# Value loads of the first attention tiles on either of two DMA queues, and new numbers in a hand-written planner

## The chip, the cores and the metric

The kernel runs on one core of a Trainium2 chip. The metric is device time in microseconds (us) of one execution. TensorE (PE) multiplies, VectorE (DVE) and ScalarE (ACT) work elementwise, GpSimd (POOL) helps them, SyncE (SP) only issues DMAs. ACT can issue DMAs too: the issue then stands in ACT's own instruction stream.

## The reference

```python
# attention: 4 x 8 heads x 576 tokens x 64; heads 0-3 see the last 32 tokens, heads 4-7 every 32nd token
scores = where(mask, scale * q @ k.T, -1e9); attn = softmax(scores); x = attn @ v
x = x.transpose(0, 2, 1, 3).reshape(2304, 512)
h = x @ w_in;  r = maximum(h, 0);  x = (s * r * r + b) @ w_out          # MLP 1, 512 -> 2048 -> 512
h = x @ w_in2; g = where(h >= 1, h, where(h <= -1, 0, (h + 1)**2 / 4))  # MLP 2
out = g @ w_out2
...
```

Everything is float32. The weights arrive as float64 and are taken apart on the chip.

## The kernel before, in words

**Tiling.** The 2304 tokens make six units of 384. Attention comes in tiles: "strided" ones (three per batch entry) and "local" ones of 256 tokens. Tiles 0 to 4 give unit 0 its tokens (0, 1, 2 strided, 3, 4 local); tile 5 is local and serves unit 1. One tile is a chain: scores on PE, maximum and subtraction on DVE, `Exp` on ACT (`sm` or `sx`), sum and reciprocal on DVE, a product on DVE or POOL, four transposes on PE, a copy `pt` on ACT or DVE, the value products on PE, and the result as a high part `xh` (ACT) and a remainder `xl` (DVE).

**MLP.** `hidden` multiplies a unit by a block of w_in, three products per tile (high by high, low by high, high by low), `output` multiplies the activated block by w_out. Each weight block of 512 KB is loaded into a `raw` or `pp` buffer, decoded (ACT L461, DVE L463 and L465) and split (ACT L442, DVE or POOL L482). A step of unit 0 needs two blocks. So the first 30 us are attention of tiles 0 to 4 beside the first loads, and the rest is a dense stream of matrix products.

**The order.** Nothing is ordered by hand after the first loads. `Issue.draw` plays the program forward with a table of costs and random due times, `order` keeps the best of 96 draws, and `emit` writes each engine's instructions in the order of the planned starts. An operation may name several engines; the planner takes the one that is free first. While PE is planned to wait before 45 us, `Pulse.run` adds dummy products (`busy`, L703 before), at most 8 in a place, to keep it active.

**Loads.** `load` (L589) issues the attention's DMAs. Up to `CALM` = 32 us of planned time, `emit` also makes each DMA on SP wait for an earlier one, so that about 2.5 planned us of bytes are under way. Apart from that the built program hands eight DMA semaphores, DMAHW0 to DMAHW7, to the DMAs in turn, in the order in which `emit` writes them; a DMA whose semaphore is still in use waits for the DMA eight places ahead of it to land. `EARLY` fixes the order in which the first tiles' loads enter the plan. Rows (queries and keys) go to `xh`/`xl` buffers, the early tiles' values to weight buffers that are still empty: tile 0 `w0hx`, tile 1 `w0lx`, tile 3 `w1hx` and `w1lx`, tile 2 `w0hx`, tile 4 `w0lx` and `w1hx`.

Of the kernel before, what the change touches and what calls it, by code (L numbers as in the profile page):

```python
# [31 lines left out]
KT = QT + STRIDE  # L32
# [12 lines left out]
FILL, MOST = 45.0, 8  # L45
# [30 lines left out]
LATENCY = 0.12  # L76
DMA_LATENCY = 2.0
DMA_ISSUE, SHORT = 0.45, 0.64
LATE, LATE_FROM, LATE_TO = 1.5, 22.0, 40.0
PIECE, PIECE_BYTE, DEEP = 0.008 / 16, 0.0435e-3 / 16, 1.0  # L80
BEGIN = {"sp": 0.7, "act": 1.4, "dve": 0.5, "pool": 6.4, "pe": 5.2}
WINDOW, PHASE, COOL, HEAT = 3.413, 2.3, 0.58, 0.9
BLOCK, FETCH, FETCH_AT, FETCH_LONG = 256, 4.5, 1.5, 1.3
CALM, FLIGHT = 32.0, 2.5
EARLY = (('rows', 0), ('rows', 1), ('w0', 0), ('vals', 0), ('rest', 0), ('rows', 3), ('vals', 1), ('rows', 4), ('vals', 3), ('vals', 2), ('vals', 4), ('w0', 1))

# [1 line left out]
class Buf:  # L88


    def __init__(self, ring, make):
        self.ring, self.make = ring, make
        self.writers, self.readers, self.users = [], [], []
        self.tile, self.left, self.end, self.near = None, 0, 0.0, 0.0
# [20 lines left out]

class Pulse:

    def __init__(self):
        self.end, self.full, self.used, self.count, self.began, self.fetched = PHASE + WINDOW, True, WINDOW, 86, 0.0, None

    def upto(self, t):
        while t >= self.end:
# [11 lines left out]
    def run(self, o, free, at, d):  # L134
        n = 0
        if at < FILL and o.fills is not None and at > free:
            self.upto(free)
            one = 0.213 if self.full else 0.427
            n = min(int(0.85 * (at - free) / one), MOST)
            self.spend(free, n * one)  # L140
        self.upto(at)
        if not self.full:
            d *= 1.85
        left = BLOCK - self.count % BLOCK
        self.count += o.count + 2 * n
        if o.count + 2 * n >= left:
            t = at + d * max(left - 2 * n, 0) / max(o.count, 1)
            self.fetched = t
            wait = max(self.began + FETCH - t, 0.0) if at < FILL else 0.0
            self.began, d = t + wait, d + wait  # L150
        self.spend(at, d)
        return n, d

# [5 lines left out]
class Issue:  # L159
# [70 lines left out]
    def draw(self, seed):  # L230
        rng = np.random.default_rng(seed)
        for ring in self.rings:
            ring.taken = []
        for o in self.ops:
            o.due = o.base + JITTER * rng.standard_normal()
            for b in o.bufs:
                b.end = b.near = 0.0
        free, pe, flight = {"port": 0.0, "dma": 0.0, "slow": 0.0}, Pulse(), []
        for o in self.ops:
            o.wait, o.ready = len(o.deps), 0.0  # L240
            for x in o.engs:
                free[x[0]] = BEGIN.get(x[0], 0.0)
            for b in o.bufs:
                b.left = len(b.users)
        pool = [o for o in self.ops if not o.wait]
        done, took = [], {}

        def room(o):
            t, more = 0.0, {}
            for b in o.allocs:  # L250
                n = len(b.ring.taken) + more.get(b.ring, 0) - b.ring.bufs
                more[b.ring] = more.get(b.ring, 0) + 1
                if n >= 0:
                    if n >= len(b.ring.taken) or b.ring.taken[n].left:
                        return None
                    t = max(t, b.ring.taken[n].near if o.engs[0][0] == "pe" else b.ring.taken[n].end)
            return t

        while pool:
            best = None  # L260
            for o in pool:
                t = room(o)
                if t is None:
                    continue
                for e, d, _, *more in o.engs:
                    at = max(free[e], o.ready, t)
                    if more and e != "pool" or "port" in more:
                        at = max(at, free[more[0]] - DEEP * (e == "sp"))
                    if e == "sp" and at < CALM:
                        at = max([at, *(end for line, end in flight if free["dma"] - line >= FLIGHT)])  # L270
                    key = (at, o.due, o.n, d)
                    if best is None or key < best[0]:
                        best = (key, o, e, d, t)
            if best is None:
                return np.inf, None
            (at, *_), o, e, d, t = best
            _, _, lag, *more = next(x for x in o.engs if x[0] == e)
            pool.remove(o)
            n = 0
            if e == "pe":  # L280
                n, d = pe.run(o, max(free[e], t), at, d)
                if pe.fetched is not None and at < FILL:
                    free["slow"], pe.fetched = max(free["slow"], pe.fetched + FETCH_AT) + FETCH_LONG, None
            took[o] = at, e, n
            free[e] = at + d
            end = at + d + lag
            if more and more[0] == "port":
                free["port"] = at + d
            elif more:
                free["dma"] = max(free["dma"], at + more[2]) + more[1]  # L290
                free["slow"] = max(free["slow"], at + more[2]) + more[1]
                end = max(at + d, free["dma"], free["slow"]) + lag + LATE * (e == "sp" and LATE_FROM < at < LATE_TO)
                if e == "sp" and at < CALM:
                    flight.append((free["dma"], end))
                    flight = flight[-12:]
            for b in o.allocs:
                b.ring.taken.append(b)
            for b in o.bufs:
                b.left -= 1
                b.end = max(b.end, end + LATENCY)  # L300
                b.near = max(b.near, at + d if e == "pe" else end + LATENCY)
            for q in o.succ:
                q.wait -= 1
                q.ready = max(q.ready, at if o in q.behind else at + d if q.engs[0][0] == e == "pe" else end + LATENCY)
                if not q.wait:
                    pool.append(q)
            done.append(o)
        assert len(done) == len(self.ops)
        return free["pe"], took
# [20 lines left out]
def sparse_attention_two_mlps(ctx: ExitStack, tc: tile.TileContext, loc, strd, w_ins, w_outs, fixed, out):  # L330
# [36 lines left out]
    class Tokens:  # L367
        def __init__(self, tag):
            self.tag, self.bufs = tag, {}
# [64 lines left out]
    def dma(n, piece, count=1, late=0.0, issue=DMA_ISSUE):  # L434
        return ("sp", issue * count, DMA_LATENCY + late, "dma", moved(n, piece), 0.0)
# [125 lines left out]
    def value_rows(src):  # L561
        (step, _), (one, n) = src.ap
        return bass.AP(tensor=src.tensor, offset=src.offset, ap=[[step, 64], [54 * step, 2], [one, n]])
# [11 lines left out]
    def is_early(i):  # L575
        return first_token(i) < U0[1]
# [9 lines left out]
            tag = "kb"  # L586
        return buf(wp if tag[0] == "w" else sp, tag, [128, 512], F32, BUFS.get(tag, MS // 2))

    def load(i, y, parts, size, piece):  # L589
        first = len(w_loads) > max(HOLD) and not held  # L590
        o = op(lambda e: [e.dma_start(out=f(), in_=x) for f, x in parts], [dma(size, piece, len(parts), issue=SHORT if len(a_line) > 2 else DMA_ISSUE)], part=[y],  # L591
               line=a_line, after=[w_loads[k] for k in HOLD] if first else ())
        if first:
            held.append(o)
            o.behind += tuple(w_loads[k] for k in HOLD)
        if i == 0 and not made[0]:
            w0_line[:] = [o]
        if is_early(i):
            w1_line[:] = [o]
        return o  # L600
# [56 lines left out]
    def vals(i):  # L657
        kind, b, d = tiles[i]
        if kind == "l":
            vs = [room(i, "vals") for _ in range(2)]  # L660
            for pos in range(2):
                for g in range(2):
                    load(i, vs[pos], [(lambda pos=pos, g=g: vs[pos].tile[half(g), :],
                                       loc[2 * d + pos][32 * g:32 * g + 64, 512 + 4 * KT:LW])], 128 * 1024, 2048)
            return vs
        vb_ = room(i, "vals")
        v4 = lambda: vb_.tile.rearrange("p (g n) -> p g n", g=2)
        if d < 2:
            for j in range(2):
                load(i, vb_, [(lambda j=j: v4()[j * 64:j * 64 + 64], value_rows(strd[b, 2 * d + j][:, VC:SW]))], 128 * 1024, 1024)  # L670
        else:
            src = strd[b, 4]
            parts = [(lambda: v4()[0:18, 0], strd[b, 3][108:126, VC:SW]), (lambda: v4()[18:36, 0], src[0:18, VC:SW]),
                     (lambda: v4()[0:64, 1], src[18:82, VC:SW]),
                     (lambda: v4()[64:118, 0], strd[b, 0:3, 108:126, VC:SW])]
            for j in range(2):
                load(i, vb_, parts[2 * j:2 * j + 2], 64 * 1024, 1024)
        return [vb_]

    def bring(i):  # L680
# [766 lines left out]
```

## Time and profile before

| | us |
|---|---|
| median of 3 runs | 823.38 (820.41 to 823.86) |
| profiled execution, its own time | 822.9 |
| its span, first to last instruction | 820.8 |
| TensorE busy in the span | 809.3 (99%) |

The profiled execution is 0.5 us under the median, and 2.1 us of it lie outside the span. The table says that PE is nearly always busy; dummy products count as busy, so the start has to be read in order of time.

### The profile page before, as it was taken

The page shows a single profiled execution, that of the slowest core. Times are in us where ns is not written, and L with a number is a line of the kernel's source. Part 1 is how long each engine was busy: PE and PEld are TensorE (multiplying, and loading weights), DVE is VectorE, ACT ScalarE, POOL GpSimd, SP SyncE. Part 2 cuts the span into 40 slices and gives each one's busy share as a digit, 9 for nine tenths or more (in the row PEclk, how much of TensorE's full clock was granted, in tenths as well). Part 3 has the DMA queues.
Part 4 walks back from the last instruction along what each step waited for, and adds up shares of the span by engine and source line. Part 5 has one row for each costly group of instructions (what it writes and reads, how often), then busy time and mean ns, then how long its engine had stood idle before and what let it go on. Part 6 is the DMA issues. An engine that isn't in the chain of part 4 may idle for free.

```text
span 820.8 us, 17686 instructions
## 1 busy us (share of the span) xinstructions
PE 809.3 (99%) x6295; PEld 783.3 (95%) x6295; DVE 629.0 (77%) x1316; ACT 517.9 (63%) x1057; POOL 103.7 (13%) x206
## 2 busy tenths in 40 slices
PE   7999999999999999999999999999999999999998
PEld 4689998999999999999999999999999999999998
DVE  5798439787777477888889988997477987466966
ACT  3486446565666576657686778855476854667553
POOL 3132103352221022221120000000000000000000
PEclk9999999999999999999999999999999999999999
DMA  7795365989777468989899999788988789878882
GB/s 238 237 335 179 101 217 195 316 267 312 259 256 267 163 227 306 329 320 332 293 315 320 300 395 351 253 251 286 296 256 254 249 255 297 288 249 255 252 271 93
DMA packets 105523, 218.23 MB, mean 266 GB/s; under 512 B 14196, under 2 KB 27868, under 8 KB 105436
## 3 DMA queue, kind: packets, MB, share of 16 engines
q1 hardware_dynamic: 95196, 180.41, 67.6%
q0 software_dynamic: 10240, 36.71, 11.9%
q8 instruction: 50, 0.82, 0.4%
q14 instruction: 37, 0.30, 0.1%
HBM read 170.93 MB, written 46.14 MB: 264 GB/s over the span
## 4 chain that ended last, share of the span: by engine, by line
PE 93%; DMA 4%; SPq 2%; DVE 0%; ACT 0%; issue 0%; ACTq 0%
PE acc L1119 8%; PE acc L1121 8%; PE acc L1120 8%; PE h L871 8%; PE h L872 8%; PE h L873 8%; PE side L1121 6%; PE side L1120 6%; PE side L1119 6%; PE acc L871 4%; PE acc L873 4%; PE acc L872 4%; PE h L1121 3%; PE h L1119 3%; PE h L1120 3%; SPq L591 2%
## 5 line engine op out<-in xcount | busy, mean ns | idle before, releaser
L871 PE MATMUL h<-xh,w0h 128*128 128x384 f32 x192 | 65.6, 342 | 0.4 <-ACT xh L442 0.4
L872 PE MATMUL h<-xl,w0h 128*128 128x384 f32 x192 | 64.6, 337 | 1.2 <-DVE xl L854 1.2
L871 PE MATMUL h<-xh,w0hx 128*128 128x384 f32 x192 | 65.6, 342 | 0.0
L873 PE MATMUL h<-xh,w0l 128*128 128x384 f32 x192 | 64.5, 336 | 0.1
L872 PE MATMUL h<-xl,w0hx 128*128 128x384 f32 x192 | 64.4, 335 | 0.0
L873 PE MATMUL h<-xh,w0lx 128*128 128x384 f32 x192 | 64.4, 335 | 0.0
L512 POOL DMA_DIRECT2D dw<-pp x60 | 43.5, 725 | 157.9 <-DVE pp L510 127.4
L903 ACT ACTIVATE t<-h 128x384 f32<-128x384 f32 x50 | 24.4, 489 | 39.0 <-PE h L873 38.6
L915 DVE TENSOR_TENSOR gg<-t,gg 128x384 fp32r<-128x384 f32 x39 | 21.6, 555 | 24.9 <-ACT gg L442 24.9
L872 PEld LDWEIGHTS h<-xl,w0h 128*128 128x128 f32 x192 | 36.1, 188 | 1.8 <-DVE xl L854 1.8
L871 PEld LDWEIGHTS h<-xh,w0h 128*128 128x128 f32 x192 | 36.0, 188 | 1.1 <-ACT xh L442 0.8
L871 PEld LDWEIGHTS h<-xh,w0hx 128*128 128x128 f32 x192 | 36.0, 188 | 0.5
L873 PEld LDWEIGHTS h<-xh,w0l 128*128 128x128 f32 x192 | 36.0, 188 | 0.4 <-DVE w0l L482 0.4
L872 PEld LDWEIGHTS h<-xl,w0hx 128*128 128x128 f32 x192 | 36.1, 188 | 0.0
L873 PEld LDWEIGHTS h<-xh,w0lx 128*128 128x128 f32 x192 | 36.0, 188 | 0.0
L442 ACT ACTIVATE gg<-w1h 128x384 fp32r<-128x384 f32 x48 | 24.9, 524 | 15.6 <-PE acc L1121 6.2
L871 PE MATMUL acc<-gg,w1h 128*128 128x384 f32 (+1 forms) x96 | 33.4, 348 | 0.2 <-DVE xl L854 0.2
L1165 DVE TENSOR_TENSOR gg<-w1h,gg 128x384 fp32r<-128x384 f32 x48 | 26.4, 554 | 8.6 <-ACT gg L442 8.1
L871 PE MATMUL acc<-gg,w1hx 128*128 128x384 f32 (+1 forms) x96 | 33.0, 344 | 0.0
L873 PE MATMUL acc<-gg,w1lx 128*128 128x384 f32 (+1 forms) x96 | 32.2, 336 | 0.0
L873 PE MATMUL acc<-gg,w1l 128*128 128x384 f32 (+1 forms) x96 | 32.2, 336 | 0.0
L872 PE MATMUL acc<-gg,w1h 128*128 128x384 f32 x96 | 32.2, 335 | 0.0
(626 smaller groups left out, 2796.2 us busy)
## 6 DMA issues: line engine op xcount, KB each, us to landing
dw<-pp POOLq DMA_DIRECT2D x60, 512.0 KB, 4.9
w0h<-dw SPq DMA_DIRECT2D x84, 256.0 KB, 3.8
w0l<-dw SPq DMA_DIRECT2D x84, 256.0 KB, 3.9
w0hx<-dw SPq DMA_DIRECT2D x84, 256.0 KB, 3.1
w0lx<-dw SPq DMA_DIRECT2D x84, 256.0 KB, 3.2
raw<-in_w_ins SPq DMA_DIRECT2D x30, 512.0 KB, 4.6
raw<-in_w_outs SPq DMA_DIRECT2D x28, 512.0 KB, 6.0
kb<-dw SPq DMA_DIRECT2D x56, 256.0 KB, 4.4
```

Of the source, the lines that this page charges most:

```text
L442: e.activation(out=out, in_=in_, func=AF.Copy)
L512: op(lambda e: e.dma_start(out=dw[o][i][qs].rearrange("q p w n -> p q (w n)"), in_=y.tile[:, 0:nq].bitcast(F32).rearrange("p q w n -> p q ...
L591: o = op(lambda e: [e.dma_start(out=f(), in_=x) for f, x in parts], [dma(size, piece, len(parts), issue=SHORT if len(a_line) > 2 else DMA_ ...
L871: e.matmul(out=acc, lhsT=wh, rhs=ah, start=first, stop=False)
L872: e.matmul(out=acc[:, 0:al.shape[1]], lhsT=wh, rhs=al, start=False, stop=False)
L873: e.matmul(out=acc, lhsT=wl, rhs=ah, start=False, stop=last)
L903: op(lambda e: e.activation(out=c(t), in_=c(p), func=AF.Relu), [act(n)], [p], [t])
L915: op(lambda e: e.tensor_tensor(out=c(gl), in0=c(t), in1=c(gh).bitcast(F32), op=SUB), [pool(n)] + [dve2(n)], [t, gh], [gl])
L1119: e.matmul(out=dst, lhsT=wh, rhs=ah, start=opens and first, stop=False, skip_group_check=not opens)
L1120: e.matmul(out=dst[:, 0:al.shape[1]], lhsT=wh, rhs=al, start=False, stop=False, skip_group_check=not opens)
L1121: e.matmul(out=dst, lhsT=wl, rhs=ah, start=False, stop=last, skip_group_check=not opens)
L1165: op(lambda e, g=g, hi=hi, lo=lo: e.tensor_tensor(out=lo.tile[:, 0:n], in0=g.tile, in1=hi.tile[:, 0:n].bitcast(F32), op=SUB), [dve2(n)], [ ...
```

## The change

Value loads of tiles that reach into unit 0 may go to ACT as well as to SP, as long as the first loads are under way (`held` is still empty); the planner picks. The order in which loads enter the plan stays. The wait of at most `DEEP` us for the DMA line now also holds for ACT's issues; the limit on bytes under way still counts SP's alone. In the planner's table, bytes on the lagging DMA engine are planned 1.2 times up to 34 us; a late landing is planned as 0.8 us between 32 and 80 us, before as 1.5 us between 22 and 40; and the fetch of PE's instructions now takes its turn on the lagging engine when a DMA is planned behind it.

```diff
-LATE, LATE_FROM, LATE_TO = 1.5, 22.0, 40.0
+LATE, LATE_FROM, LATE_TO = 0.8, 32.0, 80.0
...
-BLOCK, FETCH, FETCH_AT, FETCH_LONG = 256, 4.5, 1.5, 1.3
+BLOCK, FETCH, FETCH_AT, FETCH_LONG = 256, 1.7, 1.0, 1.3
+SLOW, SLOW_TO = 1.2, 34.0
...
-            self.fetched = t
-            wait = max(self.began + FETCH - t, 0.0) if at < FILL else 0.0
-            self.began, d = t + wait, d + wait
+            if self.fetched is not None and at < FILL:
+                self.free["slow"] = max(self.free["slow"], self.fetched) + FETCH_LONG
+                self.coming, self.fetched = self.free["slow"] + FETCH, None
+            wait = max(self.coming - t, 0.0) if at < FILL else 0.0
+            d += wait
+            self.fetched = t + wait + FETCH_AT
...
-                        at = max(at, free[more[0]] - DEEP * (e == "sp"))
+                        at = max(at, free[more[0]] - DEEP * (e in ("sp", "act")))
...
-                free["slow"] = max(free["slow"], at + more[2]) + more[1]
+                if pe.fetched is not None and pe.fetched <= at < FILL:
+                    free["slow"] = max(free["slow"], pe.fetched) + FETCH_LONG
+                    pe.coming, pe.fetched = free["slow"] + FETCH, None
+                free["slow"] = max(free["slow"], at + more[2]) + more[1] * (SLOW if at < SLOW_TO else 1.0)
...
-    def load(i, y, parts, size, piece):
+    def load(i, y, parts, size, piece, also=False):
         first = len(w_loads) > max(HOLD) and not held
-        o = op(lambda e: [e.dma_start(out=f(), in_=x) for f, x in parts], [dma(size, piece, len(parts), issue=SHORT if len(a_line) > 2 else DMA_ISSUE)], part=[y],
+        ways = [dma(size, piece, len(parts), issue=SHORT if len(a_line) > 2 else DMA_ISSUE)]
+        if (also and is_early(i)) and not held:
+            ways.append(("act", *ways[0][1:]))
+        o = op(lambda e: [e.dma_start(out=f(), in_=x) for f, x in parts], ways, part=[y],
```

The four calls of `load` in `vals` pass `True` for `also`. What this makes of the two queues' streams is shown at three places (the last number of a name is the buffer's).

SP before, from the last rows of tile 3 to the second weight block; `xh3` and `xl3` are tile 4's rows, `w...` are values, `raw_22` is the weight block:

```order
L591 DMA xl4_11_269<-in_loc 128x896
L591 DMA w0lx_12_279<-in_strd 64x2x256 x2
L591 DMA xh3_13_303<-in_loc 128x896
L591 DMA xl3_14_309<-in_loc 128x896
L591 DMA w1hx_15_339<-in_loc 64x512 x2
L591 DMA w1lx_16_366<-in_loc 64x512 x2
L591 DMA w0hx_17_414<-in_strd 18x256 x2
L591 DMA w0hx_17_414<-in_strd 64x256
L591 DMA w0hx_17_414<-in_strd 54x1x256
L591 DMA w0lx_18_471<-in_loc 64x512 x2
L591 DMA w1hx_19_499<-in_loc 64x512 x2
L457 DMA raw_22_528<-in_w_ins 128x512
```

The same stretch of SP after the change, with the semaphores that each DMA waits for:

```order
L601 DMA xl4_11_273<-in_loc 128x896 [waits DMAHW2_49]
L601 DMA xh3_13_282<-in_loc 128x896 [waits DMAHW0_49]
L601 DMA xl3_14_310<-in_loc 128x896 [waits DMAHW6_49,DMAHW1_49]
L601 DMA w1hx_15_340<-in_loc 64x512 [waits DMAHW7_49,DMAHW2_49]
L601 DMA w1lx_16_393<-in_loc 64x512
L601 DMA w0hx_17_420<-in_strd 64x256
L601 DMA w0hx_17_420<-in_strd 54x1x256 [waits DMAHW3_49]
L464 DMA raw_22_523<-in_w_ins 128x512 [waits DMAHW4_49]
```

Between tile 4's last rows and the weight block stand four DMAs where there were twelve.

ACT after the change, from the second half of tile 3's `w1lx` to the `Exp` of tile 2; `sm_50` is tile 3, `pt_37` tile 1, `sx_42` tile 2:

```order
L601 DMA w1lx_16_393<-in_loc 64x512 [waits DMAHW5_49]
L601 DMA w0hx_17_420<-in_strd 18x256 [waits DMAHW6_49]
L601 DMA w0hx_17_420<-in_strd 18x256 [waits DMAHW7_49]
L601 DMA w0lx_18_428<-in_loc 64x512 [waits DMAHW1_49]
L793 ACTIVATE sm_50_350<-sm_50_350 128x4x128 [waits DVE_49,Activation_49,Pool_49]
L601 DMA w0lx_18_428<-in_loc 64x512 [waits DMAHW3_49]
L449 ACTIVATE pt_37_432<-h_36_431 128x512 [waits PE_49]
L601 DMA w1hx_19_443<-in_loc 64x512 [waits DMAHW5_49]
L601 DMA w1hx_19_443<-in_loc 64x512 [waits DMAHW7_49]
L793 ACTIVATE sx_42_402<-sx_42_402 128x4x128 [waits DVE_49,Pool_49]
```

Before, ACT held only the three activations here, in the order `pt_37`, `sx_42`, `sm_50`. Eleven of its instructions are now DMA issues, the first ahead of all softmax work and the others between the softmax steps of tiles 0 to 2, and tile 5's scores stand ahead of the first `hidden` on PE where they stood inside it.

## Rows read from the trace of the kernel before

**Rows 1.** Windows of the whole span: busy us of each engine, clock, DMA share, GB/s.

```profile
core 0: us, PE busy (x) PEld busy (x) DVE busy (x) ACT busy (x) POOL busy (x), PEclk, DMA share, GB/s
32.00:50.00 18.00, 15.81 (x201) 12.99 (x202) 15.31 (x31) 12.66 (x27) 4.35 (x7) 1.00 1.00 335
...
700.00:800.00 100.00, 100.00 (x578) 100.00 (x577) 68.07 (x133) 64.30 (x129) 0.00 (x0) 1.00 0.83 261
```

**Rows 2.** TensorE in order of time: start, length, what, [idle before <- releaser].

```profile
19.78 0.62 PE L769 MATMUL acc<-xl 64*32 64x64 f32 x32 [0.59 <-DMA xl<-in_loc]
...
21.38 2.85 PE L703 MATMUL h<-idb_t 128*128 128x512 bf16 x8
...
30.05 1.47 PE L703 MATMUL h<-idb_t 128*128 128x384 bf16 x8
...
33.39 0.44 PE L872 MATMUL h<-xl,w0h 128*128 128x384 f32 x1 [1.04 <-DVE xl L854]
34.37 0.39 PE L749 MATMUL acc<-bias_t,idb_t 128*128 128x256 bf16 x2
35.52 0.45 PE L871 MATMUL h<-xh,w0h 128*128 128x384 f32 x1
38.78 1.90 PE L703 MATMUL h<-idb_t 128*128 128x512 bf16 x8
41.20 0.63 PE L795 MATMUL h<-id_t,sx 128*128 128x128 f32 x4 [0.52 <-DVE sx L786]
41.59 0.42 PE L871 MATMUL h<-xh,w0h 128*128 128x384 f32 x1
43.00 0.71 PE L821 MATMUL acc<-pt,qx 64*64 64x32 f32 x30 [0.25 <-ACT pt L442]
47.31 0.44 PE L871 MATMUL acc<-gg,w1h 128*128 128x384 f32 x1 [0.25 <-DVE xl L854]
```

**Rows 3.** SyncE's DMA issues in order of time.

```profile
13.33 0.35 SPq L591 DMA_DIRECT2D xl<-in_loc  x1
17.66 1.14 SPq L591 DMA_DIRECT2D w1hx<-in_loc  x2
...
20.85 2.22 SPq L591 DMA_DIRECT2D w0hx<-in_strd  x4
...
24.31 2.09 SPq L591 DMA_DIRECT2D w1hx<-in_loc  x2
26.45 0.60 SPq L457 DMA_DIRECT2D raw<-in_w_ins  x1
```

**Rows 4.** SyncE's queue: waited for what, us in total, times, longest.

```profile
SPq L591 <- DMA w0lx<-in_strd: 3.9, 1, 3.9
```

**Rows 5.** Windows of the start and the first unit, columns as in Rows 1.

```profile
16.00:20.00 4.00, 2.13 (x101) 1.50 (x100) 2.81 (x9) 1.38 (x3) 0.11 (x1) 0.99 0.52 176
20.00:24.00 4.00, 4.00 (x72) 2.17 (x53) 3.44 (x12) 1.54 (x6) 2.04 (x2) 0.58 0.40 112
...
48.00:60.00 12.00, 12.00 (x128) 11.15 (x127) 11.90 (x23) 10.40 (x21) 5.08 (x12) 1.00 0.96 305
60.00:76.00 16.00, 16.00 (x193) 14.57 (x193) 15.93 (x37) 12.41 (x33) 5.72 (x7) 1.00 0.56 192
```

**Rows 6.** ScalarE in order of time.

```profile
19.63 0.62 ACT L783 ACTIVATE sm<-sm 128x512 f32<-128x512 f32 x1
...
23.43 0.63 ACT L783 ACTIVATE sm<-sm 128x512 f32<-128x512 f32 x1 [1.23 <-DVE sm L780]
...
30.68 0.68 ACT L461 ACTIVATE dt<-raw 128x512 f32<-128x512 f32 x1 [2.32 <-DMA raw<-in_w_ins]
31.25 0.77 ACT L442 ACTIVATE xh<-acc 128x128 fp32r<-128x128 f32 x4
```

**Rows 7.** VectorE in order of time.

```profile
25.31 0.68 DVE L784 TENSOR_REDUCE mx<-sm 128x8 f32<-128x520 f32 x1
...
35.70 0.76 DVE L777 TENSOR_REDUCE mx<-acc 128x4 f32<-128x256 f32 x2 [1.77 <-PE acc L769]
```

More of the change, by code (lines that the diff above doesn't have):

```diff
@@ L116, with __init__ @@
 class Pulse:
-    def __init__(self):
-        self.end, self.full, self.used, self.count, self.began, self.fetched = PHASE + WINDOW, True, WINDOW, 86, 0.0, None
+    def __init__(self, free):
+        self.free = free
+        self.end, self.full, self.used, self.count, self.coming, self.fetched = PHASE + WINDOW, True, WINDOW, 86, 0.0, None
     def upto(self, t):
@@ L237, in draw @@
                 b.end = b.near = 0.0
-        free, pe, flight = {"port": 0.0, "dma": 0.0, "slow": 0.0}, Pulse(), []
+        free, flight = {"port": 0.0, "dma": 0.0, "slow": 0.0}, []
+        pe = Pulse(free)
         for o in self.ops:
@@ L281, in draw @@
                 n, d = pe.run(o, max(free[e], t), at, d)
-                if pe.fetched is not None and at < FILL:
-                    free["slow"], pe.fetched = max(free["slow"], pe.fetched + FETCH_AT) + FETCH_LONG, None
             took[o] = at, e, n
@@ L663, in vals @@
                     load(i, vs[pos], [(lambda pos=pos, g=g: vs[pos].tile[half(g), :],
-                                       loc[2 * d + pos][32 * g:32 * g + 64, 512 + 4 * KT:LW])], 128 * 1024, 2048)
+                                       loc[2 * d + pos][32 * g:32 * g + 64, 512 + 4 * KT:LW])], 128 * 1024, 2048, True)
             return vs
@@ L669, in vals @@
             for j in range(2):
-                load(i, vb_, [(lambda j=j: v4()[j * 64:j * 64 + 64], value_rows(strd[b, 2 * d + j][:, VC:SW]))], 128 * 1024, 1024)
+                load(i, vb_, [(lambda j=j: v4()[j * 64:j * 64 + 64], value_rows(strd[b, 2 * d + j][:, VC:SW]))], 128 * 1024, 1024, True)
         else:
@@ L676, in vals @@
             for j in range(2):
-                load(i, vb_, parts[2 * j:2 * j + 2], 64 * 1024, 1024)
+                load(i, vb_, parts[2 * j:2 * j + 2], 64 * 1024, 1024, True)
         return [vb_]
```

## The prediction

> **What bounds the kernel now.** I read the windows of the span first. From 48 us on TensorE has no idle time to give back: 12.00 of 12 us and 16.00 of 16 busy up to 76 us [rows 5], 100.00 of 100 near the end [rows 1]. What an edit of the first loads can win lies ahead of that, where idle PE and dummy products (L703) are the loss. In order of time [rows 2]: the dense products start at 33.39, when VectorE delivers the last `xl` of tile 4. Behind that PE still loses 2.4 us from 38.78 to 41.20 (eight dummies, then a wait), about 0.9 us between 41.59 and 43.00 (a stretch with three products of about 0.17 us) and 0.25 us ahead of 47.31: 3.5 us in all.
>
> SyncE's queue says why the loads are late. From 13.68 to 17.66 it waits for `w0lx`, 3.9 us [rows 4], then issues twelve value DMAs one behind the other until the second weight block goes out at 26.45 [rows 3]. While it does, the DMA engines are busy for 0.52 and 0.40 of the time [rows 5]: the stretch is bound by issue and by waits, not by bytes. The late block shows on ScalarE, which idles 2.32 us until it lands at 30.68 and holds up `xh` of tile 4 [rows 6], and late rows of tile 5 leave DVE idle for 1.77 us ahead of 35.70 [rows 7].
>
> Behind 34 us DVE is almost as full as PE: 11.90 of 12 and 15.93 of 16 us [rows 5]. A start without waits for loads can only use up DVE's idle time.
>
> **The change, part by part.**
>
> *SP's stream.* `xh3` no longer stands behind two issues of `w0lx`. `xl3` waits for `xh4` and `k3` as before, so it goes out near 12.8 instead of 13.33; its landing ends PE's wait at 19.78 [rows 2, 3]. With less queued ahead I put it at 19.0, bounds 17.5 (the idle half of the DMA time put to use) and 19.7 (nothing gained). Then four issues where twelve took 26.45 - 17.66 = 8.8 us, the last of which waits for `xh3`: the second weight block leaves at about 18.6 instead of 26.45. Tile 5's rows and the next blocks follow it, some 7 us early.
>
> *What that is worth.* It removes ACT's 2.32 us wait and DVE's 1.77. PE's 3.5 us of later loss is not all to be had, since DVE has the same work to do. Its idle time from 32 to 50 us is 18 - 15.31 = 2.7 us, 1.77 of it this wait, and from 48 to 76 us 0.2 [rows 1, 5, 7]. Work done, in DVE's time, bounds the gain at about **-2.8 us**; below it the bound is 0.
>
> *ACT's stream.* The eleven issues stand in ACT's own order. ACT does not pass one that waits, so the softmax work behind it waits too. The rows of the order name the semaphores. Taken in turn, DMAHW6 of the first `w0hx` issue is that of `xl3`. Thus ACT stands still until `xl3` lands, about 19.0. No row prices an issue on ACT; the nearest are SP's, 2.22/4 = 0.55 to 2.09/2 = 1.05 us each [rows 3], and I take 0.6 because most pairs are near the low end. Behind the landing:
> - three issues, 1.8: `Exp` of tile 3 at 20.8, done 21.4 (before it started at 19.63 [rows 6]);
> - one issue and `pt` of tile 1, 0.6 each: 22.6;
> - two issues, 1.2: `Exp` of tile 2 at 23.8.
>
> Before, the last `Exp` ahead of tile 4's was at 19.63, tile 4's at 23.43: 3.8 us for sum, maxima and subtractions [rows 6]. The order on DVE again puts tile 4's maxima behind the sum of the tile ahead, so tile 4's `Exp` comes at 23.8 + 3.8 = 27.6. From there to the dense products it was 33.39 - 23.43 = 9.96 us. Two pieces fall away: tile 4's values were out at 30.05 and `xh` began at 31.25, behind the decode that waited for its block, 1.2 us [rows 2, 6]; and DVE began tile 4's sum at 25.31, 1.25 us after its `Exp` ended at 24.06, because it had a `pt` copy in hand that ACT does now [rows 6, 7]. New start: 27.6 + 9.96 - 1.2 - 1.25 = 35.1.
>
> *Tile 5.* Its scores now stand ahead of the first dense product, where PE waits anyway; before they took 35.52 - 34.37 = 1.15 us inside it [rows 2]. So 35.1 is to be compared with 33.39 + 1.15 = 34.5: **+0.6 us**. Bounds: -4.2 (ACT is never held, below) and +4.0 (1.05 us per issue for six issues, +2.7, and `xl3` at 19.7, +0.7).
>
> *The clock.* PE was busy 2.13 of 4 us from 16 to 20, and from 20 to 24 its granted clock was 0.58, part of it at 1.2 GHz; eight dummies took 2.85 us there, and 1.90 us at 2.4 GHz [rows 2, 5]. With ACT late, PE has less to do from 18 to 30, and more of tiles 1 to 4 may run at 1.2 GHz. One such price, 0.95 us for 1.9 us of work, is the size of it; most falls where PE waits: **+0.5 us**, bounds 0 and 1.7.
>
> *The planner's numbers.* LATE, FETCH and SLOW issue nothing. They and the draws move the order of everything behind; with PE full from 48 us on they cost what PE loses there anew. I put it at 0, bounds -0.2 and +0.5.
>
> The Trainium skill has a rule against the whole change (DMA: Bandwidth & Descriptors, "Issuing engines are not separate DMA queues"): issues from SP and ACT end on the same DMA engines, and issuing on both saves only the sequencer's issue time, usually small beside the transfer. The trace does not show it small here: the queue is busy for 8.8 us while the engines idle about half. By the rule the loads would be no earlier and the -2.8 would drop out, which is the second rival.
>
> **The sum.** -2.8 + 0.6 + 0.5 = -1.7 us against the profiled execution's own 822.9: **821.2**. Against the median of 823.4 it would be 821.7; the 0.5 us between them is less than the three runs differ.
>
> **The rivals.**
>
> *ACT is not held (faster).* The idle DMA time from 16 to 24 speaks for it [rows 5]: if everything lands about 1.5 us earlier, tile 3's `Exp` comes at 19.0, tile 4's at 22.8, and the dense products start at 22.8 + 9.96 - 1.2 - 1.25 = 30.3, 4.2 us under 34.5. Half of the -2.8 is then used up already, since DVE has less time to prepare weight blocks: -4.2 - 1.4 = -5.6, **817.3**. Against it: ACT's six issues behind `xl3` cost their 3.6 us even when every wait is over.
>
> *Issue is not the limit (no gain).* If the two queues take turns in issuing, or bytes bind after all, the second weight block lands near 30 as before. The -2.8 goes, the waits on ACT stay: +0.6 + 0.5 = +1.1, **824.0**. Against it: the 3.9 us wait ahead of 17.66 is gone in any case [rows 4].
>
> *ACT becomes the bound of the start (slower).* Each issue on ACT costs 1.05 us, `xl3` lands at 19.7, and the clock is low when the dense products start (+1.7 instead of +0.5): -1.7 + 2.7 + 0.7 + 1.2 = +2.9, **825.8**. It decides where the dense products start after 36.8: 34.5 plus the 2.8 of earlier loads, less the clock's 0.5. Two more waits of 1 us on ACT take it over +4.1.
>
> **How the numbers follow.** My forecast 0.42, ACT not held 0.20, no gain 0.20, slower 0.18. A change of 0.5% is 4.1 us, about what a measurement of this kernel can tell from none. Only the first rival passes it below (with a tail of the forecast, 0.21), and most of the slow rival above (0.13); the rest, 0.66, is within it. The range goes from 817.0, a little under the first rival, to 826.0, a little over the third, and leaves out a tail at either end. The likeliest case alone is 819.5 to 823.
>
> **What would show it.** Right: the second weight block issued near 18.6 and landed by 23; ACT with DMA issues that end when `xl3` lands; tile 3's `Exp` near 21, tile 2's near 24, tile 4's near 27.6; dense products from about 35; less than 1 us of PE's idle time and dummies behind them; DVE nearly full from then on. Wrong: `Exp` of tile 4 before 24 (ACT is not held), dense products before 32 or after 38, the second block issued after 23, a granted clock under 1.00 beyond 34, or new idle time of PE behind 48 us.

## The result, and the profile after

| | median us | runs | ratio to before (95% interval) |
|---|---|---|---|
| before | 822.67 (820.41 to 824.85) | 10 | |
| after | 827.91 (825.16 to 832.43) | 10 | 1.0063 (1.0046 to 1.0080) |

The change costs 5.2 us. The forecast was 821.2 with a range from 817.0 to 826.0. The profiled execution of after took 825.16 us (span 823.4), the shortest of its ten, so its trace shows less of the loss than there is.

ScalarE in order of time, after (ACTq rows are its DMA issues; behind the operation, in brackets, the idle time and what ended it):

```profile
18.54 1.40 ACTq L601 DMA_DIRECT2D w0hx<-in_strd  x2
19.98 0.49 ACTq L601 DMA_DIRECT2D w0lx<-in_loc  x1
20.60 0.63 ACT L793 ACTIVATE sm<-sm 128x512 f32<-128x512 f32 x1 [5.53 <-DMA w0hx<-in_strd]
...
23.59 0.63 ACT L793 ACTIVATE sx<-sx 128x512 f32<-128x512 f32 x1 [1.34 <-DVE sm L796]
...
27.49 0.63 ACT L793 ACTIVATE sm<-sm 128x512 f32<-128x512 f32 x1 [0.58 <-DVE sm L790]
...
30.29 0.68 ACT L468 ACTIVATE dt<-raw 128x512 f32<-128x512 f32 x1
...
475.64 0.49 ACT L449 ACTIVATE pp<-side 128x384 f32<-128x384 f32 x1 [2.38 <-DMA dw<-pp]
```

VectorE, after:

```profile
16.89 0.74 DVE L790 TENSOR_TENSOR sm<-acc,mx 128x256 f32<-128x256 f32 x2
...
21.26 0.69 DVE L794 TENSOR_REDUCE mx<-sm 128x8 f32<-128x520 f32 x1 [2.96 <-ACT sm L793]
...
29.36 0.42 DVE L864 TENSOR_TENSOR xl<-acc,xh 128x256 fp32r<-128x256 f32 x1 [0.52 <-ACT xh L449]
29.70 0.19 DVE L795 RECIPROCAL mx<-mx 128x8 f32<-128x8 f32 x1
```

The first issue of `w0hx` leaves at 18.54, when `xl3` has landed. For 5.53 us, from 15.07 to 20.60, ScalarE computes nothing: it waits at DMA issues or makes them. Not all of that is loss. The subtraction for tile 3's `Exp` ends on VectorE at 17.63, so the issues hold this `Exp` up by 3.0 us. The three `Exp` stand at 20.60, 23.59 and 27.49, where the forecast put 20.8, 23.8 and 27.6 (before, those of tiles 3 and 4 stood at 19.63 and 23.43 [rows 6]). The second weight block is decoded at 30.29 with no wait, where ScalarE had waited 2.32 us for it [rows 6]. But it had landed at 22.48 and lay there: ScalarE comes to it only 0.39 us earlier than before (30.68 [rows 6]).

SyncE's issues, after:

```profile
12.19 0.33 SPq L601 DMA_DIRECT2D xl<-in_loc  x1
...
17.49 0.39 SPq L464 DMA_DIRECT2D raw<-in_w_ins  x1
```

The block is issued at 17.49 instead of 26.45 [rows 3], 1.1 us ahead of the forecast.

TensorE, after:

```profile
22.30 1.22 PE L821 MATMUL side<-pt,w0lx 54*64 54x54 f32 x32 [3.94 <-ACT pt L449]
...
36.18 0.47 PE L881 MATMUL h<-xh,w0h 128*128 128x384 f32 x1
36.62 0.44 PE L882 MATMUL h<-xl,w0h 128*128 128x384 f32 x1
...
39.70 0.33 PE L883 MATMUL h<-xh,w0l 128*128 128x384 f32 x1 [1.05 <-issue]
...
41.98 0.61 PE L713 MATMUL h<-idb_t 128*128 128x512 bf16 x2
...
67.29 0.80 PE L821 MATMUL side<-pt,qv 54*64 54x54 f32 x32 [0.83 <-DVE sx L790]
...
479.09 0.44 PE L1129 MATMUL side<-tm,w0l 128*128 128x384 f32 x1 [1.60 <-DVE cpx L451]
```

The second dense product starts at 36.62 (before 33.39 [rows 2], forecast 35.1). Behind it PE loses 1.05 + 0.61 us, before 3.5. New are two waits in the dense stream, 0.83 us at 67.29 and 1.60 us at 479.09. The second goes back to the last ACT row above: a copy into `pp` waits 2.38 us for the store that still reads this buffer, and the copies behind it on ScalarE and VectorE come late.

Windows of after:

```profile
16.00:20.00 4.00, 2.35 (x43) 1.31 (x34) 2.12 (x7) 0.00 (x0) 0.11 (x1) 1.00 1.04 258
20.00:24.00 4.00, 1.70 (x37) 1.19 (x37) 2.16 (x5) 1.64 (x3) 0.00 (x0) 0.59 0.88 254
24.00:28.00 4.00, 4.00 (x93) 2.52 (x92) 2.89 (x10) 1.93 (x7) 1.04 (x1) 0.56 1.00 288
60.00:76.00 16.00, 15.05 (x214) 13.35 (x213) 16.00 (x41) 13.33 (x34) 4.72 (x8) 1.00 0.71 234
470.00:490.00 20.00, 18.40 (x106) 17.87 (x105) 17.38 (x34) 16.10 (x34) 2.24 (x4) 1.00 1.03 393
```

The DMA engines, busy for 0.52 and 0.40 of the time from 16 to 24 before [rows 5], are now busy for 1.04 and 0.88 of it. The granted clock is low from 20 to 28 (0.59, 0.56) where before it was low from 20 to 24 alone (0.58 [rows 5]). The window behind that, before:

```profile
24.00:28.00 4.00, 4.00 (x105) 3.23 (x103) 2.82 (x8) 1.61 (x8) 0.11 (x1) 1.00 0.58 166
```

**Progress.** The 4,248 dense products come in nearly the same order in every version, so the start of the n-th shows where time goes. The table gives it for before, in us, and the difference to it in the profiled executions of others; each is one execution. The labels are explained below.

| n | before | after | e6 | e8 | e10 | e11 | e12 | e9 | e16 |
|---|---|---|---|---|---|---|---|---|---|
| 0 | 31.91 | +4.27 | +4.70 | +5.43 | -0.54 | +5.58 | +6.02 | +0.22 | -1.52 |
| 48 | 48.45 | -0.13 | +2.95 | +1.34 | -1.13 | +0.24 | +0.56 | -3.12 | -2.01 |
| 200 | 81.95 | +0.65 | +3.70 | +2.12 | -0.38 | +0.63 | +1.10 | -2.36 | -2.02 |
| 2250 | 470.40 | +0.53 | +3.19 | +3.68 | -0.80 | +1.24 | +1.74 | -2.85 | -2.63 |
| 2300 | 479.07 | +2.57 | +5.83 | +4.84 | +1.49 | +1.24 | +1.74 | -0.24 | -2.63 |

In after's profiled execution the start has lost nothing by product 48 and the rest loses 2.7 us, 0.8 of it by product 200 and 2.0 around 475 us.

### The profile page after: what moved, and what is told of

Read it like the earlier page. It is cut to its first block, busy times and chain, and to the rows that moved or that the text cites. A ratio compares the mean times of both kernels' runs of the same rounds, so it can differ in the third digit from the quotient of the medians.

```text
span 823.4 us, 17679 instructions
## 1 busy us (share of the span) xinstructions
PE 810.3 (98%) x6299; PEld 784.5 (95%) x6299; DVE 620.4 (75%) x1304; ACT 521.2 (63%) x1066; POOL 111.5 (14%) x209
## 4 chain that ended last, share of the span: by engine, by line
PE 88%; DMA 4%; issue 4%; DVE 1%; ACT 1%; ACTq 0%; POOL 0%; SPq 0%; POOLq 0%
PE h L881 8%; PE h L882 8%; PE h L883 8%; PE acc L1131 7%; PE acc L1129 7%; PE acc L1130 7%; PE side L1129 5%; PE side L1131 5%; PE side L1130 5%; PE acc L881 4%; PE acc L883 4%; PE acc L882 4%; PE h L1131 3%; PE h L1130 3%; PE h L1129 3%
## 5 line engine op out<-in xcount | busy, mean ns | idle before, releaser
L1175 DVE TENSOR_TENSOR gg<-w1h,gg 128x384 fp32r<-128x384 f32 x48 | 26.3, 554 | 10.4 <-ACT gg L449 10.3
```

What stands on the lines that cost most here:

```text
L1175: op(lambda e, g=g, hi=hi, lo=lo: e.tensor_tensor(out=lo.tile[:, 0:n], in0=g.tile, in1=hi.tile[:, 0:n].bitcast(F32), op=SUB), [dve2(n)], [ ...
```

## The experiments

Two theories. **Start**: what happens ahead of 48 us costs the time, with ScalarE held at DMA issues. **Order**: the new plan also puts the operations behind 48 us in an order in which PE waits. All were timed against before. Where the text below takes the difference of two ratios, its interval reaches about 2 us to either side, an estimate from the intervals of the two.

| | what | median us | n | ratio (95% interval) |
|---|---|---|---|---|
| e1 | numbers, no issue on ScalarE | 825.43 | 8 | 1.0035 (1.0023 to 1.0048) |
| e2 | issues on ScalarE, old numbers | 825.84 | 6 | 1.0050 (1.0035 to 1.0065) |
| e3 | after + 14 dummies | 829.82 | 6 | 1.0085 (1.0065 to 1.0105) |
| e5 | after, other draws | 824.95 | 6 | 1.0038 (1.0023 to 1.0052) |
| e6 | after again | 827.51 | 6 | 1.0057 (1.0037 to 1.0076) |
| e7 | before, one load on ScalarE | 822.99 | 12 | 1.0007 (0.9989 to 1.0025) |
| e8 | after, one copy moved | 827.74 | 10 | 1.0064 (1.0043 to 1.0085) |
| e9 | after's plan, no issue on ScalarE | 824.91 | 12 | 1.0033 (1.0011 to 1.0054) |
| e10 | old start, new rest | 825.63 | 12 | 1.0041 (1.0023 to 1.0058) |
| e11 | new start, old rest | 824.88 | 12 | 1.0034 (1.0016 to 1.0051) |
| e12 | new start without issues, old rest | 824.40 | 12 | 1.0023 (1.0006 to 1.0040) |
| e13 | before, other draws | 823.83 | 12 | 1.0022 (1.0004 to 1.0040) |
| e14 | e11, issues behind `Exp` | 831.40 | 6 | 1.0097 (1.0076 to 1.0118) |
| e15 | e12, second block early | 823.63 | 12 | 1.0003 (0.9987 to 1.0020) |
| e16 | before, second block early | 822.56 | 12 | 0.9986 (0.9968 to 1.0005) |

### The halves of the change (e1, e2)

e1 is after without the way over ScalarE (its diff below), e2 is before with the change's edits of `load` and `vals` and of the `DEEP` line alone; each makes its own plan.

```diff
-        if (also and is_early(i)) and not held:
+        if False and also:
```

> The changed kernel with ScalarE's way for the value loads taken out; the planner's new numbers stay. Two theories. Start: the changed kernel is slower because eleven DMA issues stand in ScalarE's stream and hold the first softmax steps, with TensorE at 1.2 GHz behind them. It expects this kernel within 1.5 us of before (ratio 0.998 to 1.002), TensorE's dense products from about 33.5 us. Order: the new plan puts waits behind 48 us (in the changed kernel's profile 0.8 us at 67 and 1.6 us at 478), and any new plan does so with other places. It expects a difference of 0.5 to 2.5 us of either sign that comes from places behind 48 us.

> The kernel before with ScalarE's way for the value loads, and the planner's old numbers. Start expects most of the slowdown: 3 to 5 us over before (ratio 1.004 to 1.006), the Exp of tile 3 not before 20 us and the dense products not before 35. Order expects it within 2 us of before, with what it loses behind 48 us.

Each half alone is slower than before, by 2.9 and 4.1 us; together they cost 5.2. The 2.9 is more than either theory expected of e1 (Start within 1.5, Order at most 2.5; its interval goes from 1.9 to 4.0), the 4.1 is what Start expected of e2. The new numbers issue nothing, so e1's loss can only come from the plan that they lead to.

### The low clock (e3)

```diff
+            for _ in range(14 if i == 1 else 0):
+                e.matmul(out=pv[0].bank.rearrange("p (a b) -> p a b", b=128), lhsT=idb_t,
+                         rhs=idb_t.unsqueeze(1).to_broadcast([128, 4, 128]), start=True, stop=True)
```

> The changed kernel, same plan, with 14 more dummy products ahead of tile 1's value products, where TensorE stood idle from 18.35 to 22.30 us. Start, as far as the clock goes, expects the granted clock at 1.00 from 20 to 27 us (0.59 and 0.56 in the changed kernel), the dense products 0.5 to 1 us earlier, the median 1 to 3 us under the changed kernel (about 825 to 827) and a narrower spread of its runs than 825 to 832. Order expects no difference beyond 0.5 us, since nothing behind 48 us moves.

The time is 829.8 against 827.9, which is not clear of noise, and no gain shows. The granted clock from 20 to 24 us is 1.00 instead of 0.59, but then it is 0.72 from 24 to 28 and 0.85 from 28 to 32: the low stretch came later, it did not go. In this execution `xl3` also landed late, at 21.19, and tile 3's `Exp` ran at 22.71. Dummies there don't pay; what the low clock costs by itself is not measured.

### Other draws (e5, e13)

```diff
-        rng = np.random.default_rng(seed)
+        rng = np.random.default_rng(seed + 1000)
```

> The changed kernel with another 96 random draws: the same loads on ScalarE and the same start, another order behind it. Start expects 825 to 828, at most the 2.4 us of the waits at 67 and 478 less than the changed kernel. Order expects it anywhere from 822 to 829, and the differences from the changed kernel behind 48 us.

> The kernel before with the random due times of its 96 draws taken from other seeds, and nothing else changed. Theory Order, in its general form (any new plan behind 48 us is a draw of a lot, and the kernel before holds a good one): 824 to 826.5, with new waits of TensorE behind 48 us. Theory Start: 822.4 to 823.4, since the loads and their queue are the same.

Nothing but the random due times differs, and after becomes 2.1 us faster (by the ratios, 0.0063 - 0.0038, of 823 us), before 1.8 us slower. The draws alone move the time by about as much as the whole forecast gain of 1.7. They move the start as well (the first dense product comes 2.4 us later than in after, and 2.5 later than before), so this is not the order behind 48 us alone. e5's time lies where Order put it, and at the lower end of Start's range. e13's median missed the lower end that Order expected by 0.2 us; its interval goes from 0.3 to 3.3.

### One load that runs ahead (e6, e7)

ScalarE issues tile 0's second value load at 1.20 us, though the plan has it at 6.1: nothing in its stream holds it back, and it overtakes tile 1's rows. A theory came up that this delays the first loads.

e6, on the plan of after (`both` holds the value loads that have two ways):

```diff
+        both = [o for o in self.ops if len(o.engs) > 1 and o.engs[1][0] == "act" and o.engs[0][3:4] == ("dma",)]
+        both[0].eng, both[0].start = "sp", both[1].start
```

> The plan and the order on every engine of the changed kernel, but tile 0's first value load (w0hx, issued by ScalarE at 1.20 us, ahead of tile 1's rows xl) goes back to SyncE behind the first weight block, where it stood before the change. Theory First load: its bytes ahead of xl and of the first weight block are why most executions start late. xl lands by about 8.6 us instead of 9.5 to 10.3, the first weight block by 10.1 instead of 11.1 to 11.7, tile 4's rows (xl3) by 19, and the time is 825 to 826 (827.9 for the change), with a spread of 3 us or less. Rival Hold: ScalarE stands still until xl3 lands whatever comes first, and the time stays at 827 to 829 with the spread of 7 us.

The edit took the wrong one of tile 0's two loads, which was on SyncE anyway, so no instruction moved: e6 is after again. As that it is of use. It repeats the time, 827.51, and its profiled execution, 829.43 us, is the longest of its six where that of after was the shortest of ten. e7, on the plan of before (`lead` is the other half of tile 0's values, of the same size, `ahead` tile 1's rows):

```diff
+        self.lead.eng, self.lead.start = "act", self.ahead.start - 1e-6
...
```

> The kernel before, its plan and its order on every engine, but tile 0's first value load is issued by ScalarE ahead of tile 1's rows xl, and nothing else. Theory First load: xl lands at 9.5 to 10.3 instead of 8.5, the first weight block at 11 to 11.7 instead of 10.0, SyncE's next rows wait for that, and the time rises by 1 to 2.5 us to 823.5 to 825. Rival Hold: one issue of 0.8 us on an idle ScalarE costs nothing, 822.4, within 0.5.

Ratio 1.0007, and the rows that the theory expected at 9.5 to 10.3 landed at 8.10 (before, 8.50): the theory falls. One issue on an idle ScalarE costs nothing that shows, though the interval, up to 2.1 us, does not exclude a cost.

### The wait at 479 us (e8)

On the plan of after, the copy that waits and the sum that reads it stand behind the next operations of their engines.

```diff
...
+        held = next(o for o in act if o.start > 471.0 and o.allocs and o.allocs[0].ring.name == "pp")
+        pp = held.allocs[0]
+        user, reader = pp.users[1:3]
+        held.start = act[act.index(held) + 2].start + 0.01
+        user.start = dve[dve.index(user) + 1].start + 0.01
+        reader.start = max(reader.start, user.start + 0.01)
```

> The changed kernel with two instructions moved near 476 us: ScalarE's copy into pp, which waits 2.4 us for a store, stands behind the next two ScalarE operations, and the VectorE sum that reads it stands behind one VectorE operation. Theory Order (the new plan puts waits on TensorE behind 48 us): the 1.6 us of TensorE's wait there go, 826.0 to 826.7 against 827.9, and in the profile no wait of more than 0.3 us between 470 and 490. Rival (the wait comes back later, since stores and loads are full there): no change, 827.5 to 828.5.

PE's wait of 1.60 us is gone there, and one of 0.46 remains. Between products 2250 and 2300 the profiled execution loses 1.2 us instead of 2.0 (after) or 2.6 (e6), but it lost 1.6 us elsewhere between products 200 and 2250, and the median did not move, as the rival expected. Undecided: what the copy costs by itself was not measured.

### All loads back on SyncE (e9)

```diff
...
+        for o in both:
+            o.eng = "sp"
```

> The plan of the changed kernel, with every value load put back on SyncE at its planned place (the first one behind the first weight block), so that ScalarE issues no DMA. Theory Hold: ScalarE is free when tile 3's scores are, Exp of tile 3 near 19.7 instead of 20.6 to 23, and the time is 824 to 825.5 though the second weight block goes out near 25. Theory First load: what the hold costs is small once the first load is back, and the time is that of the run with only the first load moved back, within 0.7 us. Rival (the earlier weight block is worth its 2.8 us): 827 to 828.5, slower than that run by 2 us.

824.91, 2.5 us under after by the ratios and what theory Hold expected. The profiled execution, 822.39, is the shortest of its twelve. ScalarE, e9:

```profile
16.15 0.63 ACT L797 ACTIVATE sm<-sm 128x512 f32<-128x512 f32 x1 [2.58 <-DVE sm L794]
...
18.27 0.63 ACT L797 ACTIVATE sx<-sx 128x512 f32<-128x512 f32 x1 [1.00 <-DVE sx L794]
...
21.82 0.63 ACT L797 ACTIVATE sm<-sm 128x512 f32<-128x512 f32 x1 [1.24 <-DVE sm L794]
...
27.30 0.66 ACT L472 ACTIVATE dt<-raw 128x512 f32<-128x512 f32 x1 [3.81 <-DMA raw<-in_w_ins]
```

Without issues in ScalarE's stream the three `Exp` come 4.5 to 5.7 us earlier than in after. Some is given back: the second weight block goes out late again, at 23.18, and ScalarE waits 3.81 us for it. The second dense product still comes 4.1 us earlier than in after (32.53 against 36.62). In after it is the other way round, the block is there and the softmax is late.

### Crosses of the two plans (e10, e11, e12)

A table gives every operation its start, engine and dummies: those that one plan starts ahead of 48 us from that plan, all others from the other. e10 is old start and new rest, e11 the reverse, e12 is e11 with all value loads on SyncE.

```diff
-        took, flight, line = self.order(), [], 0.0
+        took, flight, line = {o: tuple(x) for o, x in zip(self.ops, json.loads(zlib.decompress(base64.b64decode(TABLE))))}, [], 0.0
```

> A cross of the two plans: every operation that the kernel before plans ahead of 48 us stands on the engine and in the order of the kernel before, all others in the order of the changed kernel. Theory Order (the new plan's order behind 48 us costs what the trace of after shows at 67 and 478 us, 2.4 to 2.7 us): 825 to 826, with TensorE waiting about 0.8 us near 67 and 1.6 us near 478. Theory Start (the whole loss comes from the first 48 us): 822.4 to 823.4, as the kernel before.

> The opposite cross: ahead of 48 us the changed kernel with its DMA issues on ScalarE, behind it the order of the kernel before. Theory Order: 825 to 825.8, that is 2 to 3 us under the changed kernel, and no wait of TensorE over 0.3 us behind 60 us. Theory Start: 827 to 828, as the changed kernel. If both hold in part, the two crosses' differences to the kernel before add up to that of the changed kernel, 4.6 to 5.2 us.

> As the last, but with all value loads on SyncE at their planned places. If ScalarE's issues cost 3 us (827.7 with them, 824.9 without, under the new plan) and the new order behind 48 us 2.5, this has neither: 822 to 823, the kernel before within 0.7. If ScalarE's issues cost nothing of themselves, it is as the last run, 825 or more. If the earlier weight block is worth anything, the last run is the faster one.

The new rest alone costs 3.4 us (1.9 to 4.8), the new start alone 2.8 (1.3 to 4.2); their sum, 6.2, is after's 5.2 within the intervals. Both theories hold in part: each interval excludes zero, and which part is the larger can't be told. PE's waits behind the first unit, e10:

```profile
PE side L1133 <- DVE cpx L455: 1.6, 1, 1.6
...
PE side L825 <- DVE sx L794: 0.9, 1, 0.9
```

and every wait of PE in the whole of e11 but that for the first constants (the first two lie in the start):

```profile
PE side L825 <- ACT pt L453: 5.1, 1, 5.1
PE acc L768 <- DMA xl<-in_strd: 1.3, 1, 1.3
...
PE side L763 <- DVE sm L794: 0.3, 1, 0.3
PE acc L1133 <- DMA kb<-dw: 0.2, 1, 0.2
```

The two waits of after come with the new rest, whichever start stands ahead of it. Between products 2250 and 2300, where the longer one lies, the new rest loses 2.0, 2.6, 2.3 and 2.6 us (after, e6, e10, e9), the old rest nothing in any of six traces (e7, e11, e12, e14, e15, e16). Counted from product 48 on, the picture is less clean. The new rest loses 2.7, 2.9, 2.6 and 2.9 us up to product 2300, the old one 1.0, 1.0 and 1.2 (e7, e11, e12), but 3.0 and 4.1 in e14 and e15 and -0.6 in e16: what the stream loses later depends on its start too.

e12, expected within 0.7 us of before, took 1.9 more; without issues on ScalarE the new start does not have its early block either. ScalarE, e12:

```profile
31.02 0.66 ACT L472 ACTIVATE dt<-raw 128x512 f32<-128x512 f32 x1 [6.97 <-DMA raw<-in_w_ins]
```

The block went out at 24.87, 1.7 us later than in e9, and its decode comes 3.7 us later than there, as much as the two executions are apart at product 48. Why the block took longer to land is not shown.

### The hold and the early block apart (e14, e15, e16)

`o[n][0]` is the planned start of operation n: 29 is the second weight block, 23 to 28 are the values of tiles 2 and 4, 89 is `Exp` of tile 2. The edits are changes of the table. e14, on e11's table:

```diff
+o[29][0] = o[89][0] + 0.0001
+for k, n in enumerate((23, 25, 26, 27, 28)):
+    o[n][0] = o[89][0] + 0.001 * (k + 1)
+o[24][0] = o[23][0] + 0.0005
```

e15 on e12's table and e16 on that of before:

```diff
+o[29][0] = o[25][0] - 1e-4
```

> As the cross with the new start and the old rest (824.9), but ScalarE's six last issues (tile 2's first values, tile 4's values) stand behind Exp of tile 2 instead of ahead of Exp of tiles 3 and 2; the second weight block goes out ahead of them. Theory Hold (ScalarE, standing at a DMA issue until the rows xl3 land, makes Exp of tile 3 run at 20.6 to 22.3 where its data are there by 16.2): Exp of tile 3 before 19, tile 2 by 21, tile 4 by 25, the dense products start 2 to 3 us earlier, and the time is 822 to 823.3. Rival Bytes (the loads take their time on the DMA engines whoever issues them, and the values of tiles 2 and 4 are late next): 824.5 to 826.

> As the cross with the new start, no issue on ScalarE and the old rest (824.4), but the second weight block goes out ahead of tile 4's values, four issues earlier on SyncE, near 20.5 instead of 23 to 25. Theory Block (without the hold it is the second weight block that ScalarE waits for, up to 3.8 us): the block lands by 25, no wait of ScalarE for it over 1 us, 821 to 822.5. Rival Bytes (tile 4's values become late instead by as much): 824 to 825.

> The kernel before, with its whole plan, but the second weight block goes out ahead of tile 4's values, four issues earlier on SyncE. It is the forecast's term for the earlier loads by itself. Theory Block: it lands near 26.5 instead of 30.6, ScalarE's wait of 2.3 us for it goes, 820 to 821.2. Rival Bytes: tile 4's values land 2 us later and hold PE instead, 822 to 823.5.

e14 went the wrong way, 831.4. ScalarE, e14:

```profile
24.21 0.93 ACTq L605 DMA_DIRECT2D w0hx<-in_strd  x2
25.18 1.46 ACTq L605 DMA_DIRECT2D w0lx<-in_loc  x2
30.79 1.12 ACTq L605 DMA_DIRECT2D w1hx<-in_loc  x2
32.54 0.63 ACT L453 ACTIVATE pt<-h 128x512 f32<-128x512 f32 x1
```

The hold was not taken away, it moved. The issues again wait for earlier DMAs, the last pair until 30.79, and behind them `pt` of tile 3 waits until 32.54; PE stands still for 9.1 us. So a held ScalarE does cost time, but what it costs in after is not measured by this run.

e15 is 1.6 us faster than e12 by the ratios, e16 1.2 us faster than before (from 2.6 faster to 0.4 slower). Both medians, 823.63 and 822.56, miss what theory Block expected, and e16's lies where the rival put it. In e15 ScalarE still waits 1.94 us for the block, until 26.70. ScalarE, SyncE and PE in e16, whose profiled execution, 820.19, is 2.4 us under its median:

```profile
21.33 0.63 ACT L797 ACTIVATE sm<-sm 128x512 f32<-128x512 f32 x1 [1.34 <-DVE sm L794]
...
21.71 0.43 SPq L468 DMA_DIRECT2D raw<-in_w_ins  x1
...
27.10 0.67 ACT L472 ACTIVATE dt<-raw 128x512 f32<-128x512 f32 x1
...
24.51 0.57 PE L825 MATMUL side<-pt,w0hx 54*64 54x54 f32 x20 [1.50 <-DMA w0hx<-in_strd]
...
30.73 0.44 PE L886 MATMUL h<-xl,w0h 128*128 128x384 f32 x1
```

The decode no longer waits, and the second dense product starts at 30.73 instead of 33.39. Not all of these 2.7 us are the moved DMA's: tile 4's `Exp` was 2.1 us ahead of before's (21.33 against 23.43 [rows 6]) when the block went out. e10 has the same start without the move, and its `Exp` stands at 21.83. ScalarE and PE, e10:

```profile
30.15 0.66 ACT L472 ACTIVATE dt<-raw 128x512 f32<-128x512 f32 x1 [2.96 <-DMA raw<-in_w_ins]
...
32.84 0.44 PE L886 MATMUL h<-xl,w0h 128*128 128x384 f32 x1 [1.04 <-DVE xl L868]
```

Against it e16 gains 2.1 us at the second dense product, 0.5 of them there before the move. So the traces speak for a gain of some 1.6 us by moving one DMA on SyncE; but an interval that ends at 1.0005 does not show that e16 beats before.

## Why the prediction was wrong, step by step

**What bounds the kernel: right in the main.** SyncE's stream held up the second block, and ScalarE waited for it. One row was misread: VectorE's 1.77 us ahead of 35.70 ended with PE's scores of tile 5, and PE came to these straight from the dense products, without waiting for rows:

```profile
34.73 0.46 PE L769 MATMUL acc<-xh 64*32 64x64 f32 x32
35.00 0.59 PE L769 MATMUL acc<-xl 64*32 64x64 f32 x32
```

**SP's stream: right for the block, wrong for the rows.** The block left at 17.49 (forecast 18.6). `xl3` landed at 18.5 in the profiled execution, inside the bounds of 17.5 to 19.7, but later than them in three others with the same start. ScalarE's first held issue, which shows that landing, and `Exp` of tile 3, in e6:

```profile
19.96 0.88 ACTq L603 DMA_DIRECT2D w0hx<-in_strd  x2
...
21.48 0.63 ACT L795 ACTIVATE sm<-sm 128x512 f32<-128x512 f32 x1 [6.43 <-DMA w1lx<-in_loc]
```

in e8:

```profile
20.21 0.86 ACTq L609 DMA_DIRECT2D w0hx<-in_strd  x2
...
21.71 0.63 ACT L801 ACTIVATE sm<-sm 128x512 f32<-128x512 f32 x1 [6.51 <-DMA w1lx<-in_loc]
```

and in e11:

```profile
20.61 1.07 ACTq L605 DMA_DIRECT2D w0hx<-in_strd  x2
...
22.32 0.63 ACT L797 ACTIVATE sm<-sm 128x512 f32<-128x512 f32 x1 [7.27 <-DMA w1lx<-in_loc]
```

Before, `xl3` was issued at 13.33 and ended PE's wait at 19.78 [rows 2, 3]. In after and e6 it was issued at 12.19 and 12.48, in e8 and e11 at 13.48 and 13.29, so the earlier issue did not always come, and where it came it did not always mean an earlier landing: the DMA engines are full from 16 to 20 in after (1.04). By the Trainium skill (DMA: Bandwidth & Descriptors, "Issuing engines are not separate DMA queues") DMAs of both engines interleave on the same DMA engines, and issuing on two saves only the issue time. The trace agrees: the rows gained little or nothing beside full DMA engines, and what was saved is SyncE's time, so that the block went out 9 us earlier.

**What that is worth, -2.8: right in kind, the size not shown.** In after's trace the gain is there: the second dense product comes 3.2 us late, product 48 0.1 us early, so 3.4 us are made up, 2.2 of them beyond the 1.15 us of tile 5's scores that went ahead. Had without issues on ScalarE, the early block is worth 1.2 us (e16) and 1.6 us (e15 against e12); both intervals take in zero.

**ACT's stream, +0.6: right in mechanism, too small.** The three `Exp` came within 0.2 us of where they were put, up to that of tile 4 at 27.49, partly by luck: `xl3` landed 0.5 us ahead of 19.0, and the three issues behind it took 2.06 us instead of 1.8. From there to the second dense product it took 9.1 us, not 7.5: VectorE took the sum at once, but its reciprocal, at 29.70, stood behind an `xl` that waited for ScalarE, so the 1.25 us did not fall away. So the second dense product is 3.2 us late, 2.1 beyond tile 5's 1.15, where the forecast had 0.6 and 0.5 for the clock. With `xl3` at 19.9 to 20.6 tile 3's `Exp` is 0.9 to 1.7 us later again, the second dense product 0.4 to 1.3. e11 against e15, both with an early block and the old rest, puts the issues on ScalarE at 2.6 us (0.0031 of 823).

**The clock, +0.5: not settled.** The low stretch grew as expected (0.59 and 0.56 from 20 to 28); e3 moved it and did not remove it, so its price stays open.

**The planner's numbers, 0 with bounds -0.2 and +0.5: this is the step that failed.** The order behind 48 us costs 3.4 us by e10 and 2.4 by after against e11 (0.0063 - 0.0034); 2.0 to 2.6 of them lie between products 2250 and 2300 in four traces. I took "PE is full from 48 us on" as a reason for nothing to happen. It is the reason for the opposite: where PE waits 0.4 us in all behind 50 us, as before, a new order has next to nothing to win. New idle time of PE behind 48 us even stood among the signs of being wrong, without a price. Five new plans were run whole, and in each profiled execution PE loses time from product 48 to 2300: 2.7 us (after), 3.1 (e1), 3.1 (e2), 1.3 (e5), 1.0 (e13, which changes nothing but the draws). The last is no more than e7 loses with before's order, though e13 has a wait of 1.5 us at 69.79 that before has not.

So the sum was -1.7 for the start and 0 for the rest; the runs say +2.8 (1.3 to 4.2) and +3.4 (1.9 to 4.8). The start missed by more, 4.5 us, but within the bounds that its terms were given; the rest left its bounds. The slow rival, ScalarE as the bound, had the right place, but its decision point, dense products past 36.8, was just missed in the profiled execution (36.62) and passed in e6, e8 and e11 (37.05, 37.77, 37.93), and no rival had a price for the rest. How the start's loss divides stays partly open. e11's trace shows 1.2 us of the 2.8 at product 2300 (its execution, 823.84, is 1.0 under its median), and 0.2 at product 48. The way over ScalarE, its issues and its early block together, costs 0.9 us under the old rest (e11 against e12) and 2.5 under the new one (after against e9), and the difference is within what these runs can tell. Why single executions of one start differ so much (product 48 at -3.12 in e9 and +0.56 in e12) was not tried, beyond the late block of e12.

## What to carry to other kernels

Where a planner writes the order, any edit of its costs re-orders the whole program: cost the rest as a new draw, by what PE waits there now (if that is next to nothing, it can hardly fall), and pin the rest, as the crosses do, before judging the edit. A DMA issue on a computing engine is part of its stream: look up which semaphore each issue waits for, and count everything behind it as late until that DMA lands. Before a second queue is opened, try the one transfer that is late ahead of those that are not (e16 speaks for it and does not prove it).

## What the runs showed of the hardware

- ScalarE computed nothing for 5.53 to 7.27 us (after, e6, e8, e11) while it stood at DMA issues whose semaphores were still in use or made them; for the last 3.0 to 4.6 us of that the operands of its next `Exp` were ready. The issues themselves took 0.40 to 0.62 us each in after, the very first 0.76.
- A DMA planned for 6.1 us on ScalarE went out at 1.20 in after, since nothing ahead of it in that stream waited; a planned start holds nothing back.
- The same stretch of program to product 48 ended 3.7 us apart in two executions (e9, e12), and the whole times of e9 reach from 822.39 to 831.10.
